# Turning keys and receptances as half-array blocks into one shared PSUM pair, in a fused linear-attention and token-mixing kernel

## The chip, the cores and the metric

The kernel runs on one core of a Trainium2 chip. The metric is the device time of one execution in microseconds (us), the median of the runs shown. Engines are named as in the profile: PE is TensorE (PEld its weight loads), DVE VectorE, ACT ScalarE, POOL GpSimd, SP the engine that issues most DMAs.

## The reference

The inputs are r, k, v and w of 4 batches, 8 heads, 768 steps and 48 channels, and a bonus u for each head and channel. A state of 48 by 48 is carried along the steps of each head:

```python
for t in range(S):
    cur = np.einsum('bhd,bhe->bhde', u[None] * kt, vt)
    y[:, :, t] = np.einsum('bhd,bhde->bhe', rt, state + cur)
    state = wt[:, :, :, None] * state + np.einsum('bhd,bhe->bhde', kt, vt)
```

The heads are then laid side by side to x (4 x 768 x 384), and a token mixer follows:

```python
wq = x @ w_q; wk = x @ w_k
W_tok = scale * np.einsum('bsd,btd->bst', wq, wk)
mixed = np.einsum('bst,btd->bsd', W_tok, x)
return (np.maximum(mixed, 0.0) @ w_out)
```

## The kernel before

Time is cut into chunks of C = 128 steps, and two chunks make a unit of 256 steps. Each of the 4 batches has three units, so there are twelve, numbered n = 0 to 11; n = 11 is the last ("end"). `unit(n, batch)` lists all steps of one. Even units use the first buffer of a ring of two, odd units the second, which is why names such as KT_107 and KT_108 alternate.

**Loads.** Four DMAs bring w, k, r and v (wg, kg, rg, vg, line 223), each into a ring of four buffers. ScalarE takes the logarithm of w (lw, 379); casts of k and r to bf16 (k16, r16, 389) and of v (VB, 493) run on GpSimd or ScalarE.

**Decays.** TensorE sums the logarithms with constant triangles (CM) into a wide buffer of two PSUM banks (cw); ScalarE makes ep (423) and en (428) of it, the exponentials of both signs.

**Turns.** `transposed` turns k16 and r16 with the identity: eight matmuls of 128 rows each, k into one bank (kt), r into another (rt), both 2 KB of bf16. VectorE or ScalarE copies k out (ks, 265 or 259); VectorE makes qT = r times ks (462), RT = r times ep (471), and KT = k times en (476), which may run on GpSimd from ks. The first and last unit make ep, en, RT and KT in halves, one for each chunk c.

**Within a chunk.** A = KT by RT is a wide buffer, masked by VectorE into AM (535). The matmuls "VB,AM" apply it to v; "SB,RT" add what the state gives. The state's update is kd (KT turned back, 261 or 267) by VB, and SB (602). The bonus goes by "UB,qT", dd, and Vd = dd times VB (515, GpSimd). X (670 on VectorE, 668 on ScalarE) is the sum in bf16; it is the mixer's x.

**Mixer.** X is turned to XT by TensorE and a copy, for units 9 and 10 by a DMA transpose from SP's queue (699). Then "wk,XT" and "XT,wq" with the copy QK, and after a batch's third unit T and TS, mx ("QK,TS"), the relu MX (271 or 273), the output matmuls "wo,MX", the copy os (259 or 265) and a store (803).

**What sets the order.** Each `add` records a step with the steps it needs. Nothing is scheduled at build time: `ORDER` is the list of all 642 steps in the order in which they are issued, and each engine gets its own steps in that order. `WAYS` holds one letter for each step that may run in more than one way: an engine (A, D, P), or for TensorE a form (E whole array, e or c in half-array pieces); a small d is VectorE reading PSUM directly. `BANKS` gives each PSUM buffer its first bank of eight; a wide one takes two. Waits between engines follow from the buffers. Every engine works strictly through its own list, so a waiting instruction holds all behind it; SP's queue of DMAs as well.

Of the kernel before, what the change touches and what calls it, by code (L numbers as in the profile page):

```python
# [10 lines left out]
F32 = mybir.dt.float32  # L11
# [21 lines left out]
class Plan:  # L33
# [86 lines left out]
]  # L120
WAYS = (
    "PPDDPDDDPDPDDPPPPPPDDPAPPEDddPPDAAcENDEDDAPEDdPAAEAEcEAEDAPPEDdAPAEDcNDEAAAAAAAADPPEAdPP"
    "AEAEEEAEDAPAcDPPADEAEcEAEAAPPcDdPPAEDcEAEADAAAAAAAPPcDdPPDEDccNDEAAPPcAdPPAeAEcNDEDAPPcD"
    "PPPDEDcEAEAAAADADAAPAcAdPPAEDEENDDPPcAdPPDeDccNDAPPcDPPPPDPPAcNDeAADNDEDDAADDDDDDAADAADN"
    "NNNNEEENNENNNENEEEENNEN"
)
BANKS = [
# [15 lines left out]
def kernel(  # L143
# [40 lines left out]
    def const(shape, dtype, name):  # L184
# [9 lines left out]
        wg=(4, HW, F32), rg=(4, HW, F32), kg=(4, HW, F32), vg=(4, HW, F32), os=(10, 2 * DM, F32),  # L194
# [51 lines left out]
    def bank():  # L246
        return Buf("s")
# [112 lines left out]

    def unit(n, batch):
# [57 lines left out]
        for cs in fine:  # L419
            w_ = 512 * len(cs)  # L420

            def f_ep(e, cs=cs):
                nc.scalar.activation(  # L423
                    view(ep.tile, cs[0] * EW + 1, [[2 * EW, NP], [EW, len(cs)], [1, C]]),
                    sums(cs), ACT.Exp, bias=kp, scale=1.0)

            def f_en(e, cs=cs):
                nc.scalar.activation(  # L428
                    view(en.tile, cs[0] * C, [[U, NP], [C, len(cs)], [1, C]]), sums(cs), ACT.Exp,
                    bias=km, scale=-1.0)  # L430
# [429 lines left out]
```

## Time and profile before

| | us |
|---|---|
| median of 3 runs (100.25 to 101.56) | 100.32 |
| the profiled execution | 99.53 |
| its span on the chip | 97.8 |
| of it 7.34 to 80.39: VectorE's first KT to the last unit's first X | 73.05 |
| of it 80.39 to 84.99: between the last unit's two halves of X | 4.60 |

The span begins with the first instruction that the profiler shows and ends with the last. TensorE's clock was granted in full throughout (1.00). In the profile's rows the engine stands first, then the operation with what it writes and reads; "128*128 128x48" on a matmul is the stationary tile (rows times columns) and what streams through it. A matmul's own length is its whole passage, and several overlap, so its price is read from start to start. In brackets stands the engine's idle time just before, and what ended it.

### The profile page before, as it was taken

Reading aid. Unit: us, or ns where it says so; the run is one execution under the profiler, and the core shown is the slowest. Engines: PE = TensorE matmul, PEld = TensorE weight load, DVE = VectorE, ACT = ScalarE, POOL = GpSimd, SP = SyncE. Lnnn points to the kernel's source line nnn. Section 1 sums busy time; section 2 is a strip of 40 time slices with the busy share of each in tenths; the row PEclk is TensorE's granted clock in tenths of the full one; section 3 lists DMA queues with packets and bytes.
Section 4 is the critical chain, followed back from the end, with each engine's and each line's share of the span. In section 5 each row is a group of like instructions: output and inputs, shape, how many; then the busy total and the mean of one; then the engine's idle time right before and its main releaser. Section 6 shows DMA issues by size and latency. Waiting matters only on the chain.

```text
span 97.8 us, 4074 instructions
## 1 busy us (share of the span) xinstructions
PE 87.7 (90%) x1710; PEld 67.6 (69%) x1713; DVE 81.7 (83%) x142; ACT 76.0 (78%) x112; POOL 68.1 (70%) x106
## 2 busy tenths in 40 slices
PE   4996888999889899999999999999999999998940
PEld 1354677878677798877788787897787776675410
DVE  5608989999999998999898999899998996384850
ACT  5237988889799799899999999869889856806610
POOL 6659758728799998767999998999968991000000
PEclk9999999999999999999999999999999999999999
DMA  1999999999999999999999999999913695928593
GB/s 29 304 323 325 325 325 299 222 292 315 287 306 247 227 287 215 304 270 245 303 301 308 277 300 294 311 323 248 289 57 132 195 153 150 397 83 322 215 319 112
DMA packets 54914, 25.03 MB, mean 256 GB/s; under 512 B 52592, under 2 KB 53744, under 8 KB 54896
## 3 DMA queue, kind: packets, MB, share of 16 engines
q1 hardware_dynamic: 54736, 24.58, 90.6%
q8 instruction: 13, 0.21, 0.8%
q10 hardware_dynamic: 160, 0.20, 0.6%
q14 instruction: 5, 0.04, 0.1%
HBM read 19.66 MB, written 4.72 MB: 249 GB/s over the span
## 4 chain that ended last, share of the span: by engine, by line
PE 42%; DMA 18%; POOL 18%; DVE 8%; issue 4%; ACT 3%; SPq 3%; POOLq 0%; DVEq 0%; ACTq 0%
PE PS L176 42%; DMA vg<-in_v_dram 12%; POOL VB L493 7%; POOL Vd L515 6%; DMA kg<-in_k_dram 6%; SPq L223 3%; DVE os L265 2%; POOL k L389 2%; POOL KT L476 2%; POOL r L389 2%; DVE RT L471 1%; ACT en L428 1%; DVE AM L535 1%; ACT ep L423 1%; DVE qT L462 1%
## 5 line engine op out<-in xcount | busy, mean ns | idle before, releaser
L535 DVE TENSOR_TENSOR AM<-PS,US 128x1024 bf16<-128x1024 f32 x24 | 28.8, 1218 | 1.0 <-PE PS L176 0.6
L493 POOL CAST VB<-vg 64x384 bf16<-64x384 f32 x42 | 21.1, 503 | 3.2 <-DMA vg<-in_v_dram 0.9
L515 POOL TENSOR_TENSOR Vd<-VB,dd 128x768 bf16<-128x768 bf16 (+1 forms) x14 | 18.0, 1292 | 1.6 <-DVE dd L265 1.1
L428 ACT ACTIVATE en<-PS,km 128x1024 bf16<-128x1024 f32 (+1 forms) x14 | 13.6, 989 | 2.4 <-PE PS L176 2.0
L423 ACT ACTIVATE ep<-PS,kp 128x1024 bf16<-128x1024 f32 (+1 forms) x14 | 13.8, 1003 | 1.4 <-PE PS L176 1.1
L176 PE MATMUL PS<-wo,MX 128*128 128x384 bf16 x72 | 13.5, 326 | 0.5 <-DVE MX L273 0.5
L176 PEld LDWEIGHTS <-KT 48*128 48x128 bf16 (+1 forms) x288 | 10.3, 95 | 3.9 <-issue 1.7
L389 POOL CAST k<-kg 128x768 bf16<-128x768 f32 x11 | 9.0, 824 | 4.5 <-DMA kg<-in_k_dram 4.3
L379 ACT ACTIVATE lw<-wg 128x768 bf16<-128x768 f32 x12 | 10.1, 844 | 2.2 <-DVE kd L230 2.1
L176 PE MATMUL PS<-RT,KT 48*128 48x128 bf16 x192 | 9.2, 217 | 1.2 <-DVE qT L462 0.5
L176 PE MATMUL PS<-CM,lw 64*128 64x128 bf16 (+1 forms) x160 | 9.4, 230 | 0.6 <-DVE ks L265 0.4
L176 PEld LDWEIGHTS <-MX 128*128 128x128 bf16 x72 | 6.2, 97 | 4.9 <-DVE MX L273 1.3
L476 DVE TENSOR_TENSOR KT<-PS,en 128x1024 bf16<-128x1024 bf16 (+1 forms) x10 | 6.3, 631 | 3.7 <-ACT en L428 3.6
L389 POOL CAST r<-rg 128x768 bf16<-128x768 f32 x10 | 8.2, 823 | 1.2 <-DMA rg<-in_r_dram 1.1
L271 ACT ACTIVATE MX<-PS 128x768 bf16<-128x768 f32 (+1 forms) x10 | 7.6, 780 | 1.5 <-PE PS L176 1.4
L471 DVE TENSOR_TENSOR RT<-PS,ep 128x1024 bf16<-128x1024 bf16 (+1 forms) x14 | 8.4, 610 | 0.5 <-PE PS L176 0.3
L462 DVE TENSOR_TENSOR qT<-PS,ks 128x1024 bf16<-128x1024 bf16 x12 | 8.2, 680 | 0.7 <-PE PS L176 0.7
L176 PEld LDWEIGHTS <-lw 64*128 64x128 bf16 (+1 forms) x160 | 6.8, 96 | 2.3 <-issue 0.9
L670 DVE TENSOR_TENSOR X<-PS,Vd 128x768 bf16<-128x768 f32 (+1 forms) x8 | 6.8, 850 | 1.6 <-PE PS L176 1.5
L176 PE MATMUL PS<-ID,r 128*128 128x128 bf16 x96 | 7.4, 220 | 0.8 <-POOL r L389 0.7
L176 PE MATMUL PS<-Z 128*128 128x512 bf16 x16 | 6.5, 523 | 1.2 <-DVE Z L826 1.2
L259 ACT COPY os<-PS 128x768 f32<-128x768 f32 (+1 forms) x9 | 6.2, 694 | 1.8 <-PE PS L176 1.8
(77 smaller groups left out, 189.7 us busy)
## 6 DMA issues: line engine op xcount, KB each, us to landing
wg<-in_w_dram SPq DMA_DIRECT2D x12, 384.0 KB, 5.3
kg<-in_k_dram SPq DMA_DIRECT2D x12, 384.0 KB, 6.0
rg<-in_r_dram SPq DMA_DIRECT2D x12, 384.0 KB, 5.1
vg<-in_v_dram SPq DMA_DIRECT2D x12, 384.0 KB, 5.9
out_dram<-os SPq DMA_DIRECT2D x9, 384.0 KB, 2.6
out_dram<-os SPq DMA_DIRECT2D x5, 192.0 KB, 2.6
wof<-in_moe_w_out_dram SPq DMA_DIRECT2D x1, 576.0 KB, 6.2
out_dram<-os ACTq DMA_DIRECT2D x1, 192.0 KB, 2.3
```

The lines of the kernel that those rows point to most:

```text
L176: return nc.tensor.matmul(o, l, rr, start=start, stop=stop, skip_group_check=True, is_transpose=trans)
L271: nc.scalar.activation(o, i, ACT.Relu)
L379: nc.scalar.activation(view(lw.tile, 0, [[64, H], [512, 2], [1, D]]), view(g["wg"].tile, 0, [[D2, H], [D, 2], [1, D]]), ACT.Ln, bias=0.0, ...
L389: op(view(o.tile, 0, [[64, H], [512, 2], [1, D]]), view(g[src].tile, 0, [[D2, H], [D, 2], [1, D]]))
L423: nc.scalar.activation(view(ep.tile, cs[0] * EW + 1, [[2 * EW, NP], [EW, len(cs)], [1, C]]), sums(cs), ACT.Exp, bias=kp, scale=1.0)
L428: nc.scalar.activation(view(en.tile, cs[0] * C, [[U, NP], [C, len(cs)], [1, C]]), sums(cs), ACT.Exp, bias=km, scale=-1.0)
L462: lambda e: nc.vector.tensor_tensor(qT.tile, at(rt, BF16), ks.tile, ALU.mult),
L471: nc.vector.tensor_tensor(slots(RT.tile, cs, C, 0, 64), slots(at(rt, BF16), cs, C, 0, 64), slots(ep.tile, cs, EW, 65, -65), ALU.mult)
L476: on("D" if e == "d" else e).tensor_tensor(plain(KT.tile, cs), plain(at(kt, BF16) if e == "d" else ks.tile, cs), plain(en.tile, cs), ALU.mult)
L493: op(view(VB.tile, c * DM, [[1, DM]], p0=half * 64, pn=64), view(g["vg"].tile, (1 - half) * D, [[D2, H], [1, D]], p0=c * 64, pn=64))
L515: (nc.vector if e == "D" else nc.gpsimd).tensor_tensor(Vd.tile[:, cols], VB.tile[:, cols], view(dd.tile, cs[0] * H, [[1, len(cs) * H], [0, ...
L535: AMs[c] = add(("AM", n, c), "D", lambda e, c=c, A=A: nc.vector.tensor_tensor(view(AM[c].tile, 0, [[C, 8], [1, C]]), view(at(A), 0, [[C, 8 ...
```

## The change

Four things are done, and the tables ORDER, WAYS and BANKS are replaced.

1. `transposed` writes k and r into one wide buffer `kr` of two banks. Each of the eight matmuls becomes two: rows 0 to 63 and rows 64 to 127 by turns, each with a 64 by 64 piece of the identity. Chunk 0 lies in the first bank, chunk 1 in the second; in each, a head pair's k stands beside its r. What reads them (ks, qT, RT, KT) steps over the other.
2. ep, en, ks, qT, RT and KT are laid out by chunk first and head pair second, where before it was the other way; the halves of the first and last unit become separate blocks.
3. The rings of wg, rg, kg and vg have five buffers for four.
4. The DMA transposes of X must be issued after the last unit's loads.

```diff
-        wg=(4, HW, F32), rg=(4, HW, F32), kg=(4, HW, F32), vg=(4, HW, F32), os=(10, 2 * DM, F32),
+        wg=(5, HW, F32), rg=(5, HW, F32), kg=(5, HW, F32), vg=(5, HW, F32), os=(10, 2 * DM, F32),
...
+        if end:
+            for x in turned_x:
+                x["after"] += [g[z + "L"] for z in ("wg", "kg", "rg", "vg")]
...
-                    view(ep.tile, cs[0] * EW + 1, [[2 * EW, NP], [EW, len(cs)], [1, C]]),
+                    view(ep.tile, cs[0] * NP * EW + 1, [[EW, NP], [NP * EW, len(cs)], [1, C]]),
...
-        kt, rt = bank(), bank()
-
-        def transposed(name, src, step, o):
+        kr = wide()
+
+        def transposed(name, src, step, z):
             def f(e):
-                x = at(o, BF16)
+                x = at(kr, BF16)
                 for hp in range(NP):
                     for j in range(2):
-                        mm(view(x, hp * U + (1 - j) * 64, [[C, 2], [1, 64]]),
-                           src.tile[:, ds(j * 512 + hp * 128, 128)], ID16, trans=True)
-            return add((name, n), "E", f, [step, su["ID"]] + new(name[0] + "16"), o, [src])
+                        for c in range(2):
+                            rows = ds(c * 64, 64)
+                            mm(x[:, ds((c * NP + hp) * U + z * C + (1 - j) * 64, 64)],
+                               src.tile[rows, ds(j * 512 + hp * 128, 128)], ID16[rows, rows],
+                               trans=True)
+            return add((name, n), "E", f, [step, su["ID"]] + new(name[0] + "16"), kr, [src], mode=1)
...
+        def turned(z, cs=(0, 1)):
+            return view(at(kr, BF16), cs[0] * NP * U + z * C, [[U, NP * len(cs)], [1, C]])
```

What the new table moves is shown at three places. First VectorE's list at the start, from the first KT to the second AM; KT, RT and the rest are the first unit's, AM the masked products. Before:

```order
L476 TENSOR_TENSOR KT_107<-PS,en_99 128x4x128 x2
L265 COPY ks_101<-PS 128x1024
L471 TENSOR_TENSOR RT_105<-PS,ep_97 128x4x128 x2
L462 TENSOR_TENSOR qT_103<-PS,ks_101 128x1024
L535 TENSOR_TENSOR AM_0_115<-PS,US 128x1024
L535 TENSOR_TENSOR AM_0_117<-PS,US 128x1024
```

And now:

```order
L488 TENSOR_TENSOR KT_111<-PS,en_103 128x512
L264 COPY ks_105<-PS 128x1024
L488 TENSOR_TENSOR KT_111<-PS,en_103 128x512
L483 TENSOR_TENSOR RT_109<-PS,ep_101 128x512
L473 TENSOR_TENSOR qT_107<-PS,ks_105 128x1024
L483 TENSOR_TENSOR RT_109<-PS,ep_101 128x512
L547 TENSOR_TENSOR AM_0_119<-PS,US 128x1024
```

The halves of KT and RT, which stood in pairs, are apart, with ks and qT between them.

Second, VectorE's list at the last unit, from the masked product of its second chunk over the two halves of X. Before:

```order
L535 TENSOR_TENSOR AM_1_118<-PS,US 128x1024
L670 TENSOR_TENSOR X_130<-PS,Vd_114 128x384
L265 COPY os_81<-PS 128x768
L602 TENSOR_TENSOR SB_122<-PS,ep_98 128x192
L265 CAST QK_132<-PS 128x256
L670 TENSOR_TENSOR X_130<-PS,Vd_114 128x384
```

And now:

```order
L547 TENSOR_TENSOR AM_1_122<-PS,US 128x1024
L682 TENSOR_TENSOR X_134<-PS,Vd_118 128x384
L264 CAST QK_136<-PS 128x256
L614 TENSOR_TENSOR SB_126<-PS,ep_102 128x192
L264 COPY XT_128<-PS 128x384
L682 TENSOR_TENSOR X_134<-PS,Vd_118 128x384
```

An output copy (os) is gone from between the halves, and the copy of the turned first half (XT) has come there. On TensorE the two groups of six "wo,MX" matmuls that stood between the last unit's two "VB,AM" groups now stand ahead of the first: 36 of the 72 come before it, where it was 24.

Third, SP's queue of DMAs behind the last load. Before:

```order
L223 DMA vg_78<-in_v_dram 128x8x96
L803 DMA out_dram<-os_80 128x768
L803 DMA out_dram<-os_82 128x768
L699 DMA_TRANSPOSE XT_124<-X_130 128x6x128
L803 DMA out_dram<-os_79 128x768
L699 DMA_TRANSPOSE XT_123<-X_130 128x6x128
L803 DMA out_dram<-os_81 128x768
```

And now:

```order
L222 DMA vg_79<-in_v_dram 128x8x96
L711 DMA_TRANSPOSE XT_127<-X_134 128x6x128
L711 DMA_TRANSPOSE XT_128<-X_134 128x6x128
L816 DMA out_dram<-os_83 128x768
L816 DMA out_dram<-os_88 128x768
L816 DMA out_dram<-os_85 128x768
```

Both transposes of X have moved ahead of all stores.

More of the change, by code (lines that the diff above doesn't have):

```diff
@@ L84 @@
 ORDER = [
[35 rows of a table removed]
[35 rows of a table added]
 ]
 WAYS = (
[L122 to L125, printed above, removed]
+    "PPDDDPPPPPPPDDPPDPAPPDAPPEDddPPDDAccNDEAAPAEAdPAAEDEENDEAAPPEDdPPDEAEEAEDAAAAAAAAAPEAPPP"
+    "DEDEEEAEDAAAEAdPPAEAEcEAEAAPAEDdPAAEDENDEADDAAAAAAPPcDdPPAEAEENDEDAPPcDdPADEDccEAEADPPEA"
+    "dPPDEDcNDEDAAAADAADPPcDPPPDEAEENDAPPcDdPAAEDccNDDPPcDdPPPDPPAcNDeDDANDEDADADAAADDDDDDAAE"
+    "NENNENNENEENEEENNNENEEN"
 )
 BANKS = [
[7 rows of a table removed]
[6 rows of a table added]
 ]
@@ L359, in bonus @@
                        reads=[z])
+    turned_x = []
     def unit(n, batch):
@@ L428, in f_en @@
                 nc.scalar.activation(
-                    view(en.tile, cs[0] * C, [[U, NP], [C, len(cs)], [1, C]]), sums(cs), ACT.Exp,
+                    view(en.tile, cs[0] * 512, [[C, NP], [512, len(cs)], [1, C]]), sums(cs), ACT.Exp,
                     bias=km, scale=-1.0)
@@ L436, in unit @@
                 eps[c], ens[c] = x, y
-        kt, rt = bank(), bank()
-        def transposed(name, src, step, o):
+        kr = wide()
+        def transposed(name, src, step, z):
             def f(e):
-                x = at(o, BF16)
+                x = at(kr, BF16)
                 for hp in range(NP):
                     for j in range(2):
-                        mm(view(x, hp * U + (1 - j) * 64, [[C, 2], [1, 64]]),
-                           src.tile[:, ds(j * 512 + hp * 128, 128)], ID16, trans=True)
-            return add((name, n), "E", f, [step, su["ID"]] + new(name[0] + "16"), o, [src])
+                        for c in range(2):
[4 more added lines that the diff above has]
+            return add((name, n), "E", f, [step, su["ID"]] + new(name[0] + "16"), kr, [src], mode=1)
         def plain(t, cs=(0, 1)):
-            return view(t, cs[0] * C, [[1, 1024]] if len(cs) > 1 else [[U, NP], [1, C]])
+            return view(t, cs[0] * 512, [[C, NP * len(cs)], [1, C]])
+        def turned(z, cs=(0, 1)):
+            return view(at(kr, BF16), cs[0] * NP * U + z * C, [[U, NP * len(cs)], [1, C]])
         def slots(t, cs, w_, x, step):
-            return view(t, cs[0] * w_ + x, [[(3 - len(cs)) * w_, NP * len(cs)], [step, 2], [1, 64]])
-        kTs = transposed("kT", k16, k16s, kt)
-        rTs = transposed("rT", r16, r16s, rt)
+            return view(t, cs[0] * NP * w_ + x, [[w_, NP * len(cs)], [step, 2], [1, 64]])
+        kTs = transposed("kT", k16, k16s, 0)
+        rTs = transposed("rT", r16, r16s, 1)
         ks = ring("ks")
-        kss = add(("ks", n), "AD", lambda e: copy(e, ks.tile, at(kt, BF16)), [kTs], ks, [kt],
+        kss = add(("ks", n), "AD", lambda e: copy(e, plain(ks.tile), turned(0)), [kTs], ks, [kr],
                   cols=1024)
@@ L461, in unit @@
         qTs = add(("qT", n), "D",
-                  lambda e: nc.vector.tensor_tensor(qT.tile, at(rt, BF16), ks.tile, ALU.mult),
-                  [rTs, kss], qT, [rt, ks])
+                  lambda e: nc.vector.tensor_tensor(plain(qT.tile), turned(1), plain(ks.tile),
+                                                    ALU.mult),
+                  [rTs, kss], qT, [kr, ks])
         RT, KT = ring("RT"), ring("KT")
@@ L476, in f_KT @@
                 on("D" if e == "d" else e).tensor_tensor(
-                    plain(KT.tile, cs), plain(at(kt, BF16) if e == "d" else ks.tile, cs),
+                    plain(KT.tile, cs), turned(0, cs) if e == "d" else plain(ks.tile, cs),
                     plain(en.tile, cs), ALU.mult)
-            x = add(("RT", n, cs[0]), "D", f_RT, [rTs] + [eps[c] for c in cs] + new("ep"), RT, [rt, ep],
+            x = add(("RT", n, cs[0]), "D", f_RT, [rTs] + [eps[c] for c in cs] + new("ep"), RT, [kr, ep],
                     cols=512 * len(cs), half=half)
@@ L482, in unit @@
                     cols=512 * len(cs), half=half,
-                    more=dict(P=([kss], [ks]), D=([kss], [ks]), d=([kTs], [kt])))
+                    more=dict(P=([kss], [ks]), D=([kss], [ks]), d=([kTs], [kr])))
             for c in cs:
@@ L531, in f_A @@
                         mm(x[:, ds(hh * 512 + hp * C, C)],
-                           KT.tile[ds(hh * 64, D), ds((2 * hp + c) * C, C)],
-                           RT.tile[ds(hh * 64, D), ds((2 * hp + c) * C, C)])
+                           KT.tile[ds(hh * 64, D), ds((c * NP + hp) * C, C)],
+                           RT.tile[ds(hh * 64, D), ds((c * NP + hp) * C, C)])
             As = add(("A", n, c), "E", f_A, [RTs[c], KTs[c]], A, [RT, KT], mode=1)
@@ L546, in f_kb @@
                         cp = c * NP + hp
-                        x = ds((2 * hp + c) * C, C)
+                        x = ds(cp * C, C)
                         if e == "E":
@@ L701, in unit @@
                     [xs], XT, [X])
+                turned_x.append(XTs)
             else:
```

8 lines of the change are left out of this document (4 added, 4 removed), and 83 rows, old and new, of tables (BANKS, ORDER).

## The prediction

> **What bounds the kernel now.** I read the page's busy shares first, then the windows, then VectorE's waits, then the timeline of the end. The page gives for each engine its busy time, share of the span and instructions.
>
> ```profile
> PE 87.7 (90%) x1710; PEld 67.6 (69%) x1713; DVE 81.7 (83%) x142; ACT 76.0 (78%) x112; POOL 68.1 (70%) x106
> ```
>
> No share decides alone, so I cut the span where VectorE's part of the work turns: at its first product of the first unit (KT, 7.34 us) and at the two halves of the last unit's X (80.39 and 84.99 us). The columns are length, then busy time and count of each engine, the granted clock, DMA share and GB/s.
>
> ```profile
> 7.34:80.39 73.05, 68.55 (x1526) 57.17 (x1529) 69.45 (x111) 65.56 (x95) 62.80 (x85) 1.00 1.00 265
> 80.39:84.99 4.60, 4.52 (x81) 3.09 (x80) 2.30 (x4) 3.32 (x6) 0.76 (x1) 1.00 0.77 272
> 84.99:97.80 12.81, 8.51 (x81) 4.70 (x78) 7.10 (x14) 4.27 (x10) 0.00 (x0) 1.00 0.59 219
> ```
>
> In the first 73.05 us VectorE (third figure) works 69.45 us: 95%, with 73.05 - 69.45 = 3.6 us idle. ScalarE has 7.5 us free there, GpSimd 10.3 us. TensorE's 68.55 us count each matmul's whole passage, and matmuls overlap, so it is not full. VectorE bounds this stage. In the second stretch TensorE is busy 4.52 of 4.60 us and VectorE half of it: TensorE's order bounds there. The rest is a chain of short steps through all engines. What VectorE waits for in the first stage (total, times, longest):
>
> ```profile
> DVE KT L476 <- ACT en L428: 3.6, 3, 3.1
> DVE dd L265 <- PE PS L176: 0.8, 2, 0.5
> DVE qT L462 <- PE PS L176: 0.7, 2, 0.5
> DVE AM L535 <- PE PS L176: 0.6, 3, 0.2
> DVE RT L471 <- PE PS L176: 0.3, 1, 0.3
> DVE RT L471 <- ACT ep L423: 0.2, 1, 0.2
> ```
>
> The 3.1 us of the first row lie ahead of 7.34. Of the rest 0.8 + 0.7 + 0.6 + 0.3 = 2.4 us are for TensorE. This is all that a quicker TensorE, earlier loads or a lighter GpSimd can give back in this stage, whatever they save themselves.
>
> **The turns of k and r.** Eight matmuls of 128 rows by 128 columns become sixteen of 64 rows by 64, on two halves of the array in turn, for 24 turns. From TensorE's timeline (start, length, form, count):
>
> ```profile
> 26.77 0.61 PE L176 MATMUL PS<-ID,k 128*128 128x128 bf16 x8
> 27.31 0.62 PE L176 MATMUL PS<-RT,KT 48*128 48x128 bf16 x16
> 40.31 0.61 PE L176 MATMUL PS<-CM,lw 64*128 64x128 bf16 x16
> 40.76 0.39 PE L176 MATMUL PS<-RT,KT 48*128 48x128 bf16 x8
> 49.22 0.62 PE L176 MATMUL PS<-ID,r 128*128 128x128 bf16 x8
> 49.68 0.77 PE L176 MATMUL PS<-VB,AM 128*128 128x48 bf16 x24
> 83.15 0.25 PE L176 MATMUL PS<-ID,X 64*128 64x64 bf16 x6
> L176 PE MATMUL PS<-ID,X 64*128 64x64 bf16 x6 | 0.2, 190 | 0.0
> ```
>
> A turn takes 49.68 - 49.22 = 0.46 us from start to start, 57 ns a matmul. The new form has a row, the last unit's X: six in 0.25 us, one of them 190 ns, so (0.25 - 0.19)/5 = 12 ns each. Sixteen take 0.20 us: 0.26 us less, times 24 is 6.2 us. The upper bound of the price is the half-row form with 128 columns (CM, lw): (40.76 - 40.31)/16 = 28 ns, 0.45 us a turn, which saves nothing. I take the row of the same shape.
>
> A change of array shape costs too: turn k to RT, KT (whole to half rows) takes 27.31 - 26.77 = 0.54 us where turn r to VB, AM (no change) took 0.46: 0.08 us. Counted through the order of instructions, between whole, half-row and half-column forms there are 102 changes before and 124 now: 22 x 0.08 = 1.8 us back. The Trainium skill, page TensorEngine Tiling (Array Packing), section Key Properties, says that changing the tiling mode drains the engine, a rule that speaks against this change; the trace agrees, with the 0.08 us just read.
>
> The table also chooses other forms. Three more units take the running sums (CM) on whole rows:
>
> ```profile
> 16.59 1.05 PE L176 MATMUL PS<-CM,lw 128*128 128x256 bf16 x8
> 17.47 0.34 PE L176 MATMUL PS<-UB,qT 128*128 128x2 bf16 x8
> ```
>
> That is 0.88 us against 0.45, so 3 x 0.43 = 1.3 us; sixteen more whole-row turns of KT at 57 ns, in place of 32 small ones at 12 ns, are another 0.5. TensorE's net is -6.2 + 1.8 + 1.8 = -2.6 us, with 0 to +3.6 if the halves gain nothing. It reaches the end only through the 2.4 us of waits above.
>
> **VectorE's own work.** By form (busy, mean ns), the rows whose counts change:
>
> ```profile
> L670 DVE TENSOR_TENSOR X<-PS,Vd 128x768 bf16<-128x768 f32 x6 | 5.7, 947 | 0.0
> L267 DVE TENSOR_SCALAR kd<-PS 128x768 bf16<-128x768 bf16 x3 | 1.6, 546 | 0.0
> L476 DVE TENSOR_TENSOR KT<-PS,en 128x512 bf16<-128x512 bf16 x2 | 0.8, 424 | 3.3 <-ACT en L428 3.3
> L265 DVE COPY dd<-PS 128x16 f32<-128x16 f32 x6 | 1.0, 168 | 0.8 <-PE PS L176 0.8
> L273 DVE TENSOR_SCALAR MX<-PS 128x384 bf16<-128x384 f32 x5 | 2.5, 548 | 1.0 <-PE PS L176 1.0
> L471 DVE TENSOR_TENSOR RT<-PS,ep 128x1024 bf16<-128x1024 bf16 x10 | 6.9, 687 | 0.3 <-PE PS L176 0.3
> L476 DVE TENSOR_TENSOR KT<-PS,en 128x1024 bf16<-128x1024 bf16 x8 | 5.5, 682 | 0.4 <-ACT en L428 0.3
> ```
>
> Ahead of the last unit's first X it gets one X (0.95), one kd (0.55), one half KT (0.42), one dd (0.17) and one TS, which has no row there; MX is a copy of the same 384 elements, 0.55. The sum is 2.64; neighbours overlap by some 0.07 each, so +2.3 us. The memsets of kd that leave VectorE lie ahead of 7.34, where it waits 3.1 us anyway, and count nothing. GpSimd has room for them: it waits 4.3 us for kg (quoted below), the first of it ahead of its first cast, so I take nothing. The new strided reads of the pair cost nothing: RT reads its bank in runs of 64 (687 ns) as fast as KT contiguous ones (682).
>
> **The start.** The first unit's halves of ep and en now lie in separate blocks.
>
> ```profile
> 9.14 0.76 DVE L471 TENSOR_TENSOR RT<-PS,ep 128x512 bf16<-128x512 bf16 x2 [0.20 <-ACT ep L423]
> 10.43 2.35 DVE L535 TENSOR_TENSOR AM<-PS,US 128x1024 bf16<-128x1024 f32 x2
> ```
>
> Both halves of RT waited for the second ep. In the new order the first is free of it: two KT, ks, RT, qT, RT are four of 0.42 and two of 0.68, 3.04 less overlaps, some 2.65 us, so AM can start at 10.0 in place of 10.43: -0.4 us (0 if TensorE is late with A).
>
> **The end.** Between the last unit's X halves VectorE waits 1.49 us for TensorE.
>
> ```profile
> 80.04 2.11 PE L176 MATMUL PS<-wo,MX 128*128 128x384 bf16 x12
> 82.08 0.27 PE L176 MATMUL PS<-SB,IDU 128*64 128x192 bf16 x2
> 80.39 0.56 DVE L670 TENSOR_TENSOR X<-PS,Vd 128x384 bf16<-128x384 f32 x1
> 81.28 0.96 DVE L265 COPY os<-PS 128x768 f32<-128x768 f32 x1 [0.33 <-PE PS L176]
> 84.99 0.56 DVE L670 TENSOR_TENSOR X<-PS,Vd 128x384 bf16<-128x384 f32 x1 [1.49 <-PE PS L176]
> ```
>
> TensorE does twelve output matmuls (wo, MX) in that gap, 82.08 - 80.04 = 2.04 us. In the new order these stand ahead of it, in the first stage, where TensorE's net relief of 2.6 covers them (without that cover they come back as waits of VectorE, 2.0). Two changes of shape go too. The gap shrinks by 2.1, from 4.60 to 2.5. VectorE's work in it, 2.30 of the second window, loses the os copy (0.96) and gains a copy of XT (some 0.4, as half a KT above): 1.7, the lower bound of the gap, 0.8 below what I take; the upper is 4.6. From the second X on, TensorE's list is the same, so I change nothing.
>
> **Loads and SP.** A fifth buffer lets a load start a unit sooner.
>
> ```profile
> POOL k L389 <- DMA kg<-in_k_dram: 4.3, 4, 1.8
> 72.31 4.05 SPq L803 DMA_DIRECT2D out_dram<-os  x2
> 76.46 1.37 SPq L699 DMA_TRANSPOSE XT<-X  x1
> 78.92 1.33 SPq L699 DMA_TRANSPOSE XT<-X  x1
> 82.26 12.72 SPq L803 DMA_DIRECT2D out_dram<-os  x11
> ```
>
> This frees GpSimd, which has 10.3 us of slack already; by itself it is worth nothing but its share of VectorE's waits. Both transposes of X now go ahead of all stores, so the three stores that left before 78.92 queue behind them. Eleven issues took 12.72 us with waits in them; the queue has room for three more before the last copy. Cost 0, at most the length of one such issue, 12.72/11 = 1.2.
>
> **Sum.** VectorE's work +2.3; its waits for TensorE halved, -1.2 (bounds 0 and -2.4, the middle because the relief of 2.6 is as large as the waits but most of it falls beside them); start -0.4; end -2.1. Together -1.4 us: 99.53 of the profiled execution (1.73 outside its span of 97.80) becomes 98.1, and the median of 100.32, which stands 0.79 above that execution, becomes 98.9. With waits and start at their bounds the sum is -2.6 to +0.2, and the case's own range 97.7 to 100.5.
>
> **Rivals.** *The waits vanish.* Loads, GpSimd and TensorE are all lighter, and VectorE's last 1.2 us of waits go as well: 97.7. For it: every wait has an upstream reason that the change touches. Against: with 2.3 us more work at 95% busy, small gaps of another cause arise. 0.24.
>
> *The waits stay.* They are lengths of single steps, not lack of TensorE: +2.3 - 0.4 - 2.1 = -0.2, 100.1. For it: 2.4 us in eight waits, none over 0.5. 0.20.
>
> *The halves don't overlap.* TensorE gets +3.6 us; if half of it shows on VectorE (+1.8), +1.6 in all, 101.9. Against it is the 12 ns of the row above. The Trainium skill, page TensorE: Matmul & The Clock Gate, section "Wait — 56ns, not 53.3ns?", has a floor of about 25 ns from start to start however small the matmul; by it a turn would take 0.40 us and this rival would hold, but the trace's 12 ns lies below it. 0.04.
>
> *The pair is held too long: slower.* Before, k's bank was free once ks (and KT) had read it, whatever became of r. Now k and r share two banks, and the next unit's turns wait for the last of ks, qT, RT and KT, with everything behind them in TensorE's queue, AM's and SB's matmuls among it. The nearest price is TensorE's wait for ks:
>
> ```profile
> PE PS L176 <- DVE ks L265: 0.8, 2, 0.5
> ```
>
> 0.4 us each; once a unit and seen in full by VectorE, 12 x 0.4 = 4.8: 98.9 + 4.8 = 103.7. It decides from 1.4 + 2.0 = 3.4 us, 0.28 a unit. Against: in the new order k's and r's turns of a unit stand close together and may use any of four pairs. 0.12.
>
> **How the numbers follow.** The forecast has 0.40. A measurement of this kernel can tell about 2%, 2.0 us, from no change: faster is below 98.3, slower above 102.3. Faster: 0.22 of the first rival and a quarter of the forecast's 0.40 (0.6 of its 2.8 us lie below 98.3), together 0.32. Slower: 0.09 of the last rival and 0.01 of the third, 0.10. Same: 0.58. The range goes from 0.8 below the first rival, the lower bound of the gap at the end, up to the third rival: 96.9 to 101.9; past it lie most of the last rival and little else.
>
> **What would show it.** Right: turns of k or r in about 0.2 us of TensorE's timeline; VectorE busy about 71.7 us from its first KT to the last unit's first X, with about 2 us idle; the X halves some 2.5 us apart; the first AM near 10.0. Wrong: VectorE's idle in that stage at 3.6 or more, TensorE waiting for ks, qT or RT ahead of turns, wk's matmuls in the gap waiting for the transposed XT, or a last store that waits in SP's queue.

## The result and the profile after

The changed kernel takes 105.43 us (median of four runs, 105.38 to 105.59) where the kernel before takes 100.28 on the same chip. The ratio of the runs is on record as 1.0545, 95% interval 1.0498 to 1.0593 (the two medians alone give 1.051). Some runs of a kernel are over 1.5% longer than its fastest; what is said below of times and medians leaves these out. The prediction was 98.9, with 96.9 to 101.9 as its range. The change is slower, and the sign of the forecast was wrong.

The head of the page after, and the windows cut at the same three points as before (first KT, the last unit's two halves of X; columns as in the prediction):

```profile
span 103.7 us, 4374 instructions
PE 88.2 (85%) x1857; PEld 66.0 (64%) x1861; DVE 81.1 (78%) x141; ACT 78.1 (75%) x114; POOL 66.5 (64%) x105
```

```profile
8.76:88.19 79.43, 70.77 (x1660) 56.32 (x1665) 71.55 (x116) 67.67 (x98) 58.97 (x79) 1.00 0.91 238
88.19:90.93 2.74, 2.66 (x74) 2.20 (x74) 1.50 (x6) 2.07 (x4) 0.00 (x0) 1.00 1.02 391
90.93:103.70 12.77, 8.57 (x78) 4.85 (x75) 6.60 (x13) 5.13 (x11) 0.00 (x0) 1.00 0.64 240
```

Set against the three rows of before, the 5.9 us of span divide without a remainder: the first KT comes 8.76 - 7.34 = 1.42 later; VectorE works 71.55 - 69.45 = 2.10 more in the first stage; it idles 79.43 - 71.55 = 7.88 there where it idled 3.60, so 4.28 more; the gap between the X halves is 1.86 shorter; the end is the same within 0.04. 1.42 + 2.10 + 4.28 - 1.86 - 0.04 = 5.90. This is bookkeeping along one engine, not yet a cause. What VectorE now waits for (total, times, longest):

```profile
DVE KT L488 <- PE PS L175: 4.8, 2, 2.6
DVE ks L264 <- PE PS L175: 2.6, 3, 1.0
DVE KT L488 <- ACT ep L428: 1.3, 1, 1.3
DVE AM L547 <- PE PS L175: 0.9, 3, 0.4
```

The waits of dd, qT, AM and RT that the prediction meant to halve did fall by nearly half, from 2.4 to 1.3 us (AM 0.9, dd and qT 0.2 each). But KT and ks, the two readers of k's half of the pair, had no wait for TensorE before, and now they have the longest. The place of the longest is unit 4, in the timeline (start, length, engine, operation):

```profile
29.94 0.83 ACT L394 CAST r<-rg 128x768 bf16<-128x768 f32 x1 [0.54 <-DMA rg<-in_r_dram]
29.96 0.41 PE L175 MATMUL PS<-ID,k 64*128 64x64 bf16 x16
30.19 0.28 PE L175 MATMUL PS<-SB,RT 48*128 48x48 bf16 x8
30.68 1.12 ACT L428 ACTIVATE ep<-PS,kp 128x1024 bf16<-128x1024 f32 x1
31.86 0.37 PE L175 MATMUL PS<-VB,kd 128*128 128x48 bf16 x8 [0.32 <-ACT ep L428]
32.16 0.41 PE L175 MATMUL PS<-ID,r 64*128 64x64 bf16 x16
32.68 0.69 DVE L488 TENSOR_TENSOR KT<-PS,en 128x1024 bf16<-128x1024 bf16 x1 [2.23 <-PE PS L175]
33.41 1.01 ACT L258 COPY ks<-PS 128x1024 bf16<-128x1024 bf16 x1 [1.60 <-DVE KT L488]
```

k's turn is over at 30.37 and en has been ready since 29.41, yet KT starts at 32.68, 0.11 us after the end of *r's* turn (32.16 + 0.41). r's turn is late because a product that waits for ep stands ahead of it on TensorE, and ep itself stands on ScalarE behind r's cast, which waited for r's load. The chain that ended last (start, length) shows the way from SP's queue of loads to KT:

```profile
22.54 1.46 SPq L222
...
24.04 5.83 DMA rg<-in_r_dram
...
30.68 1.13 ACT ep L428
...
31.86 0.73 PE PS L175 x24
...
32.68 0.69 DVE KT L488
```

Then ks, on ScalarE, waits until KT has read the same banks. So a reader of k waits for the last writer of the shared pair that is issued ahead of it, r's turn; and two readers on different engines take turns, which is not new with the pair, since ks and KT shared k's bank before too. The Trainium skill, page PSUM — Partial Sum Buffer, section "PSUM bank collisions raise a hardware error", has a rule that asks for such waits: two engines must not be on the same bank (and the same partitions) at once, reads against reads included, even at different addresses. The waits of the trace are as this rule asks; the prediction, which drew on two other pages, missed it.

The same lies behind the wait ahead of KT in unit 6 (1.25 us; the view names ep, r's turn ends at 47.55, KT starts at 47.66) and of most of that ahead of ks in unit 5 (1.02; k's turn ends at 38.65, r's at 39.43): 4.5 us with unit 4's. Two more waits ahead of ks look alike and are not. In unit 9 (0.74) k's own turn stood still for 0.79 us in the middle, from 65.83 on, which the profiles of e3 and e8 below don't show. In unit 11 (0.82) r's turn ends only 0.23 us behind k's, and with own banks the wait is still 0.79 (e1, below).

The start, from the same timeline:

```profile
4.45 1.17 POOL L229 MEMSET kd<- 128x1280 bf16 x1
5.68 0.29 POOL L284 TENSOR_SCALAR_AFFINE_SELECT CM<-CM 64x128 bf16<-64x128 bf16 x1
6.28 0.29 POOL L284 TENSOR_SCALAR_AFFINE_SELECT CM<-CM 64x128 bf16<-64x128 bf16 x1
6.62 0.92 PE L175 MATMUL PS<-CM,lw 128*128 128x256 bf16 x7 [1.04 <-POOL CM L284]
7.65 1.27 ACT L433 ACTIVATE en<-PS,km 128x512 bf16<-128x512 f32 x2 [2.48 <-PE PS L175]
8.24 0.41 PE L175 MATMUL PS<-ID,r 64*128 64x64 bf16 x16
8.76 0.42 DVE L488 TENSOR_TENSOR KT<-PS,en 128x512 bf16<-128x512 bf16 x1 [2.58 <-PE PS L175]
```

GpSimd writes the zeros of a kd buffer before it finishes the triangles CM; the running sums wait for CM, en for the sums, and KT, once en's first half is done at about 8.28, waits for r's turn again.

### The profile page after: what moved, and what is told of

Its sections match the earlier page's. It is cut to its first block, busy times and chain, and to the rows that moved or that the text cites. A ratio compares the mean times of both kernels' runs of the same rounds, so it can differ in the third digit from the quotient of the medians.

```text
span 103.7 us, 4374 instructions
## 1 busy us (share of the span) xinstructions
PE 88.2 (85%) x1857; PEld 66.0 (64%) x1861; DVE 81.1 (78%) x141; ACT 78.1 (75%) x114; POOL 66.5 (64%) x105
## 4 chain that ended last, share of the span: by engine, by line
PE 39%; SPq 22%; DVE 13%; issue 9%; DMA 6%; POOL 5%; ACT 3%; DVEq 0%; POOLq 0%; ACTq 0%
PE PS L175 39%; SPq L222 22%; DMA rg<-in_r_dram 6%; DVE AM L547 3%; POOL VB L505 3%; POOL k L394 2%; DVE KT L488 2%; DVE ks L264 1%; DVE RT L483 1%; DVE qT L473 1%; DVE SB L614 1%; ACT ep L428 1%; ACT VB L505 1%; DVE X L682 1%; ACT os L258 1%
## 5 line engine op out<-in xcount | busy, mean ns | idle before, releaser
L505 POOL CAST VB<-vg 64x384 bf16<-64x384 f32 x40 | 20.1, 503 | 3.5 <-DMA vg<-in_v_dram 2.1
L175 PE MATMUL PS<-CM,lw 64*128 64x128 bf16 (+1 forms) x136 | 10.5, 239 | 2.3 <-POOL CM L284 1.0
L258 ACT COPY os<-PS 128x768 f32<-128x768 f32 (+1 forms) x12 | 8.2, 692 | 4.2 <-PE PS L175 4.1
L175 PE MATMUL PS<-RT,KT 48*128 48x128 bf16 x192 | 9.7, 217 | 1.5 <-DVE RT L483 1.2
L175 PEld LDWEIGHTS <-lw 64*128 64x128 bf16 (+1 forms) x136 | 7.5, 95 | 4.5 <-issue 3.4
L394 POOL CAST r<-rg 128x768 bf16<-128x768 f32 x9 | 7.4, 824 | 2.4 <-DMA rg<-in_r_dram 2.1
L682 DVE TENSOR_TENSOR X<-PS,Vd 128x768 bf16<-128x768 f32 (+1 forms) x9 | 7.7, 862 | 1.2 <-PE PS L175 1.0
L394 POOL CAST k<-kg 128x768 bf16<-128x768 f32 x10 | 8.2, 824 | 0.7 <-DMA kg<-in_k_dram 0.6
L175 PE MATMUL PS<-VB,AM 128*128 128x48 bf16 x192 | 7.8, 183 | 0.6 <-DVE AM L547 0.5
L175 PE MATMUL PS<-ID,KT 128*128 128x128 bf16 x80 | 6.7, 220 | 1.3 <-DVE KT L488 0.9
```

What stands on the lines that cost most here:

```text
L175: return nc.tensor.matmul(o, l, rr, start=start, stop=stop, skip_group_check=True, is_transpose=trans)
L258: nc.scalar.copy(o, i)
L394: op(view(o.tile, 0, [[64, H], [512, 2], [1, D]]), view(g[src].tile, 0, [[D2, H], [D, 2], [1, D]]))
L505: op(view(VB.tile, c * DM, [[1, DM]], p0=half * 64, pn=64), view(g["vg"].tile, (1 - half) * D, [[D2, H], [1, D]], p0=c * 64, pn=64))
```

## The experiments

**Theory 1**: sharing one pair makes k's readers wait for r's turn. **Theory 2**: the kd zeros on GpSimd delay the start. **Theory 3**: VectorE's longer list costs its 2.1 us. The rival to all is the new order as such. Each run stood beside runs of the kernel before on its chip; the ratio is to these, with its 95% interval. The kernel before varied between 99.5 and 101.9 there, so ratios and trace intervals are read rather than medians where less than 1 us matters.

| run | median us | ratio | interval |
|---|---|---|---|
| changed kernel | 105.43 | 1.0545 | 1.0498 to 1.0593 |
| e1 own banks | 102.31 | 1.0211 | 1.0112 to 1.0311 |
| e2 own banks, zeros on VectorE | 102.64 | 1.0232 | 1.0146 to 1.0317 |
| e3 zeros on VectorE | 104.49 | 1.0425 | 1.0346 to 1.0504 |
| e4 r's turn later, units 4 and 6 | 103.76 | 1.0372 | 1.0268 to 1.0476 |
| e5 own banks in six units | 102.87 | 1.0247 | 1.0129 to 1.0365 |
| e6 order of before, halves in 3 units | 117.03 | 1.1653 | 1.1553 to 1.1753 |
| e7 before, end in another order | 105.04 | 1.0446 | 1.0313 to 1.0578 |
| e8 four load buffers | 105.42 | 1.0467 | 1.0330 to 1.0605 |
| e9 before, new layouts, five buffers | 101.26 | 1.0103 | 0.9995 to 1.0210 |
| e10 e1, work back on ScalarE | 106.34 | 1.0743 | 1.0606 to 1.0881 |
| e11 e3 and e4 together | 102.32 | 1.0237 | 1.0132 to 1.0343 |
| e12 e2, v loaded once | 101.53 | 1.0138 | 1.0075 to 1.0200 |
| e13 all cures of order | 101.53 | 1.0073 | 1.0033 to 1.0114 |
| e14 e1 without four kd | 102.17 | 1.0148 | 1.0068 to 1.0228 |
| e15 changed, without four kd | 105.14 | 1.0387 | 1.0312 to 1.0461 |
| e16 e13, v loaded once | 100.78 | 1.0069 | 1.0027 to 1.0110 |
| e17 before, v loaded once | 99.39 | 0.9824 | 0.9712 to 0.9936 |
| e18 e14 without four turns of KT | 102.17 | 1.0193 | 1.0129 to 1.0258 |

### Sharing: e1, e4, e5

e1 undoes the sharing, and with it the half turns; the order stays, and what reads the banks follows (the edit in short):

```diff
-        kr = wide()
+        kr = [bank(), bank()]
...
-                        for c in range(2):
-                            rows = ds(c * 64, 64)
-                            mm(x[:, ds((c * NP + hp) * U + z * C + (1 - j) * 64, 64)],
-                               src.tile[rows, ds(j * 512 + hp * 128, 128)], ID16[rows, rows],
+                        mm(view(x, hp * C + (1 - j) * 64, [[NP * C, 2], [1, 64]]),
+                           src.tile[:, ds(j * 512 + hp * 128, 128)], ID16,
```

> The changed kernel's order of steps, engines, five load buffers and chunk-first layouts, but k's and r's turns go into a bank of their own each (the two banks of the pair), with whole 128-row turns as before. Theory 1 (k's readers wait for r's turn because both lie in one pair of banks; the waits in the changed trace are 2.2 us in unit 4, 1.25 in unit 6, 1.0, 0.7 and 0.8 before the ks copies of units 5, 9 and 11, sum 6.0): about 100.3 us (99.3 to 101.5), and those five waits for TensorE gone, though each turn is 0.26 us longer again. Rival (the new order itself, or the loads, cost the time): 104.5 to 106.

102.3: 3.1 us of the 5.1 expected. Its window of the first stage, and its two rows of waits (line numbers moved):

```profile
8.28:85.71 77.43, 74.20 (x1494) 59.27 (x1493) 72.29 (x117) 68.17 (x98) 59.32 (x79) 1.00 0.92 248
```

```profile
DVE ks L266 <- PE PS L177: 1.1, 2, 0.8
...
DVE KT L497 <- PE PS L177: 0.8, 3, 0.4
```

Behind the first KT, the waits of KT and ks fall from 2.2 + 2.6 + 1.3 = 6.1 us to 1.9; ahead of it VectorE still idles 2.23 us for 2.58, now for en. Unit 4's wait falls from 2.23 to 0.22, unit 6's from 1.25 to 0.38, unit 5's from 1.02 to 0.33: 3.6 us in all, close to the 3.1 us of time. Unit 11's stays at 0.79, which the expectation had counted as gone. The order alone is not to blame: the same order is 3 us faster with own banks, although every turn is longer again. VectorE's idle falls by less, 7.88 to 77.43 - 72.29 = 5.14: other waits appear.

e4 keeps pair and half turns and moves two steps in ORDER:

```diff
-    ... 156, 207, 231, 235, 245, 204, 232, 319, ...
+    ... 156, 207, 235, 245, 204, 232, 231, 319, ...
...
-    ... 257, 292, 328, 291, 293, 326, 325, 162, 332, 329, ...
+    ... 257, 292, 291, 293, 326, 325, 162, 332, 329, 328, ...
```

(231 and 328 are r's turns of units 4 and 6, 232 and 329 the ks behind which they now stand.)

> The changed kernel, shared pair and half turns kept, with r's turn of units 4 and 6 put behind the copy ks of the same unit, so that KT and ks read k's half of the pair before r's turn writes the other. Theory 1: the KT waits of 2.2 and 1.25 us go, RT behind it pays up to 0.8 us each for the later turn: about 103.5 us (102.6 to 104.5). Rival (KT waits for something else that r's turn only happens to end with): 105.0 to 106.

103.8, 1.7 less. The KT of units 4 and 6 in its timeline, which started at 32.68 and 47.66:

```profile
30.33 0.69 DVE L488 TENSOR_TENSOR KT<-PS,en 128x1024 bf16<-128x1024 bf16 x1
...
44.59 0.69 DVE L488 TENSOR_TENSOR KT<-PS,en 128x1024 bf16<-128x1024 bf16 x1 [0.22 <-ACT en L433]
```

2.35 and 3.07 us earlier, and in unit 6 what KT now waits for is en. In unit 4 r's turn itself starts at 32.12, where it started at 32.16; only KT no longer waits for it. Moving r's turn of two units and nothing else removes both waits, so it was r's turn that held KT: theory 1 holds in its mechanism, and in size for these two units.

e5 gives own banks only to units 0, 4, 5, 6, 9 and 11 (`own = n in (0, 4, 5, 6, 9, 11)`):

> The changed kernel with own banks and whole turns only in the six units where the trace shows k's readers waiting for r's turn (0, 4, 5, 6, 9, 11); the shared pair and the half turns stay in the other six (1, 2, 3, 7, 8, 10). Theory 1, in place (only where r's turn stands between k's turn and k's readers does the sharing cost): the same as with own banks everywhere, 102.3 us, or up to 0.6 less (101.5 to 102.7). Rival (sharing costs everywhere a little, by banks held longer): 103.5 to 104.5.

102.9 lies just above the expected range and below the rival's; its ratio of 1.025 is e1's 1.021 within the intervals, and below the changed kernel's. The six units hold most of the loss, though units 9 and 11 were chosen on waits that were hardly for r's turn. "Up to 0.6 less" for the shorter turns in the other six was not seen.

### The start: e3, e2, e12

```diff
-    ... 14, 21, 32, 12, 1, ...
+    ... 14, 21, 31, 32, 12, 1, ...
```

(31 and 32 are the kd zeros, their letters in WAYS changed from P to D.)

> The changed kernel with one thing of the start undone: the zeros of the two kd buffers are written by VectorE in its idle stretch from 2.1 to 5.9 us, not by GpSimd ahead of the last two masks. Theory 2 (GpSimd's list holds the masks, these the cumulative sums, these the first KT): the first KT starts 1.3 us earlier, near 7.4 us, and the time is about 104.2 us (103.9 to 104.6). Rival (the lead is lost again in a later wait for a load or for TensorE): first KT earlier, time 105.2 to 105.5.

104.5, 0.9 less. Its start:

```profile
6.68 1.27 ACT L433 ACTIVATE en<-PS,km 128x512 bf16<-128x512 f32 x2 [1.53 <-PE PS L175]
6.82 0.82 POOL L394 CAST r<-rg 128x768 bf16<-128x768 f32 x1 [0.35 <-DMA rg<-in_r_dram]
7.70 0.41 PE L175 MATMUL PS<-ID,r 64*128 64x64 bf16 x16 [0.46 <-POOL r L394]
8.21 0.42 DVE L488 TENSOR_TENSOR KT<-PS,en 128x512 bf16<-128x512 bf16 x1 [1.66 <-PE PS L175]
```

en comes 0.97 us earlier, as theory 2 says, but KT only 0.55: it now waits for r's turn, that for r's cast, that for r's load. The sharing carries the load of r into KT.

> Both in one: own banks with whole turns, and the kd zeros on VectorE, in the changed kernel's order. Theories 1 and 2 together, added: about 99.0 us (98.0 to 100.3). If only theory 1 holds: 100.3. If only theory 2: 104.2. If neither: 105.4.

102.6: with own banks the zeros bring nothing. The first KT is at 7.82 for 8.28, but unit 1's KT at 15.06 for 14.69. Between them two waits for loads have grown:

```profile
11.54 0.84 ACT L386 ACTIVATE lw<-wg 128x768 bf16<-128x768 f32 x1 [1.20 <-DMA wg<-in_w_dram]
...
12.78 2.15 POOL L514 CAST VB<-vg 64x384 bf16<-64x384 f32 x4 [2.98 <-DMA vg<-in_v_dram]
```

e12 takes eleven loads away:

```diff
+            if name == "vg" and n:
+                g[name] = vg0[0]
+                g[name + "L"] = add((name, n), "S", None)
+                continue
```

> The changed order with own banks and the kd zeros on VectorE (102.6 us), with v loaded for unit 0 alone: the other eleven units use unit 0's v, so eleven of the 48 loads (4.3 of 18.9 MB) are left out and the output is that of repeated values. Theory (the early start is lost because the first units' loads queue behind each other): the first KT stays near 7.8 us, the waits for wg and vg between 10 and 16 us go, and the time is 101.4 us (100.6 to 102.0). Rival (loads are never on the path): 102.3 to 103.0.

The time is 101.5, as expected, but not all on the way there: the first KT is at 7.13, not near 7.8, and the cast of v (VB) shown above still waits 2.02 us, for unit 0's v. From unit 5's KT to the last X, e12 and e1 in one row each:

```profile
38.03:87.04 49.01, 48.34 (x1027) 38.70 (x1027) 44.79 (x74) 42.18 (x63) 33.17 (x43) 1.00 0.49 143
```

```profile
39.45:88.48 49.03, 48.37 (x1027) 38.72 (x1027) 44.79 (x74) 42.19 (x63) 33.30 (x43) 1.00 0.82 229
```

At a DMA share of 0.49 for 0.82 this stretch is no shorter; e2's is as long (39.87 to 88.89). Unit 2's KT starts at 19.29 in e12, 20.71 in e1 and 21.12 in e2, so the lead of 1.42 us over e1 is there by then. In these kernels the loads count only ahead of that point, and a lead won there is kept in full.

### Order alone: e11, e13, and e16, e17

> The changed kernel, shared pair and half turns kept, with both cures of order: the kd zeros on VectorE and r's turn of units 4 and 6 behind ks. If the two add (each alone gave 0.9 and 1.7): 102.8 us (102.4 to 103.2). Theory (the earlier start is used up in the first units, which wait for their loads): 103.5 us (103.2 to 104.2).

102.3, below both ranges: the two cures add up, and a little more. The start was not used up here.

e13 adds four moves: r's turn of unit 0 (49) behind its second KT (55), that of unit 5 (272) ahead of a turn of X (159), unit 4's SB (248) ahead of unit 5's ks (273), unit 11's turns (545, 546) ahead of T (437).

```diff
-    ... 271, 159, 272, 273, 248, 275, ...
+    ... 271, 272, 159, 248, 273, 275, ...
...
-    ... 527, 529, 437, 522, 545, 546, 177, ...
+    ... 527, 529, 545, 546, 437, 522, 177, ...
```

> The changed kernel with shared pair and half turns, cured by order alone: kd zeros on VectorE and r's turn of units 4 and 6 behind ks (together 102.3 us measured), and besides r's turn of unit 0 behind unit 0's KT, r's turn of unit 5 ahead of the turn of X that stood between, the SB of unit 4 ahead of unit 5's ks, and unit 11's two turns ahead of the sum T over X. Theory 1 for what is left (the waits of 1.6, 1.1 and 0.8 us before KT of unit 0 and ks of units 5 and 11 are still r's turn): they fall by 0.3, 0.5 to 1.0 and 0.7, the time to 100.8 us (100.0 to 101.7). Rival (what is left over the kernel before is not sharing): 101.9 to 102.8.

101.5, and 1.007 times the kernel before: inside what was expected, and 0.047 of the 0.0545 is gone with the pair and the half turns still there. The profiled execution took 103.05, above the others, so only its start is read:

```profile
7.13 0.42 DVE L488 TENSOR_TENSOR KT<-PS,en 128x512 bf16<-128x512 bf16 x1 [0.62 <-ACT en L433]
...
8.21 0.72 PE L175 MATMUL PS<-ID,r 64*128 64x64 bf16 x16 [0.45 <-DVE ks L264]
```

The first KT is at 7.13, ahead of the kernel before (7.34). This was the best version with the pair; no version with all its work in it beat the kernel before.

> The changed kernel cured by order alone (101.4 us, and its casts and copies now wait 18 us in all for loads, on several engines side by side, where the kernel before waits 7), with v loaded for unit 0 alone; the other units use unit 0's v, eleven of 48 loads are left out. Theory (with the waits for r's turn gone, the loads set what is left): 99.8 us (99.2 to 100.6). Rival (loads are waited for only where there is time): 101.0 to 101.8.

> The kernel before with the same eleven loads of v left out (the other units use unit 0's v). Theory (its order waits for loads 7 us in all, 1.3 of it for v, beside other work): 100.2 us (99.4 to 100.7), so the loads are not what sets its time. Rival (both kernels are paced by the loads): 98.0 to 99.2.

e16 has e13's ratio (1.0069 and 1.0073): by it no gain, though its median lies between the two ranges. So in the cured kernel the loads don't set what is left. e17 lies at the border of its two. Its ratio is 0.982, but against the four shortest runs of the kernel before beside it (99.78 to 100.45, median 100.19) e17 gains only 0.8 us. So what the kernel before gains from lighter loads is open between under 1% and 2%, and neither range is confirmed.

### VectorE's list: e10, e14, e15, e18

> The changed order with own banks and whole turns (102.3 us), and three pieces of VectorE's added work back on ScalarE (the copy TS of unit 5, kd of units 1 and 3: 0.56 + 0.55 + 0.55 = 1.65 us of VectorE, 2.1 us of ScalarE), the cast of wo back on GpSimd (1.14 us of ScalarE). Theory 3 (what is left over the kernel before is VectorE's longer list, which has few gaps): 100.9 us (100.4 to 101.6). Rival (the list is paced by TensorE or the loads, the pieces only turn into waits): 102.0 to 103.

Three letters D in WAYS became A, and the cast of wo P. 106.3, far on the other side; in part this is a fault of the experiment, the cast of wo came late.

```profile
70.77 1.14 POOL L266 CAST wo<-wof 128x1152 bf16<-128x1152 f32 x1
...
71.97 1.14 PE L177 MATMUL PS<-wo,MX 128*128 128x384 bf16 x6 [2.14 <-POOL wo L266]
```

TensorE, and all behind it, stood 2.1 us; what else this run lost is open. But ahead of that it says something: unit 8's KT starts at 59.20, in e1 at 59.16, with two of the three pieces (the copies kd of units 1 and 3) already gone from VectorE. To take work away without giving it to another engine, e14 and e15 leave out four copies:

```diff
             def f_kd(e, cs=cs):
+                if n in (3, 5, 7, 8):
+                    return
```

> The changed order with own banks and whole turns (102.3 us), with the copies kd of units 3, 5, 7 and 8 left out of VectorE (4 x 0.55 = 2.2 us) and given to no other engine; the state of those units is then built from an older kd. Theory 3 (VectorE's list is what the stage waits for, each us of it counts): 100.2 us (99.6 to 100.9). Rival (the engines wait for one another, work taken from one alone turns into waits): 101.6 to 102.6.

> The changed kernel itself, with the same four copies kd left out of VectorE (2.2 us), the state of those units built from an older kd. If VectorE's work counts one for one also beside the waits for r's turn: 103.2 us (102.8 to 103.8). Rival (the stage is set by the chain of casts, turns and KT, VectorE's list has the room): 104.6 to 105.6.

From unit 2's KT to the last X, e14 and then e1:

```profile
19.86:87.61 67.75, 66.11 (x1394) 53.69 (x1394) 61.25 (x97) 59.45 (x85) 50.64 (x65) 1.00 0.90 246
```

```profile
20.71:88.48 67.77, 66.12 (x1394) 53.70 (x1394) 62.64 (x101) 59.15 (x85) 49.95 (x65) 1.00 0.89 244
```

Four copies of 0.55 us fewer (VectorE is busy 61.25 us for 62.64), 0.02 us gained: theory 3 falls for own banks. For the changed kernel the times alone are less sharp: e15 is 0.3 us shorter by the median, 1.6% by the ratios (1.0387 for 1.0545, the kernel before being slower in that round). The traces settle it from unit 4's KT to the last X, where three of the four copies lie. First e15, then e8, which is the changed kernel with four load buffers:

```profile
32.04:89.69 57.65, 53.28 (x1282) 42.58 (x1283) 51.32 (x83) 48.58 (x72) 39.96 (x53) 1.00 0.85 223
33.22:90.90 57.68, 53.29 (x1282) 42.65 (x1283) 52.10 (x86) 48.60 (x72) 39.90 (x53) 1.00 0.87 226
```

Three copies fewer, 0.03 us gained: theory 3 falls here too. (e3 takes 57.68 us for this stretch as well; the profiled execution of the changed kernel takes 58.25, with the stop of 0.79 us in unit 9.) In e14's stretch TensorE is busy 66.1 of 67.8 us, so the last run also left out the turns of KT that fed those copies:

> As the run before it with own banks, whole turns and without the copies kd of units 3, 5, 7 and 8, and now without the turns of KT (kb) that fed them: 32 matmuls, 4 x 0.46 = 1.8 us of TensorE, are left out too; the state of those units is built from an older kd. From unit 2's KT to the last X TensorE is busy 66.1 of 67.8 us in that version. Theory (with own banks TensorE's list sets the pace): 100.3 us, 1.8 less (99.8 to 100.8), and that stretch 66.0 us. Rival (TensorE's busy time counts passages that overlap, another chain sets it): 101.7 to 102.4, the stretch 67.3 to 67.8.

```profile
21.13:88.49 67.36, 64.83 (x1370) 52.62 (x1370) 61.26 (x97) 59.06 (x85) 49.14 (x64) 1.00 0.87 238
```

67.36 for 67.75 us: 0.4 of the 1.8 (TensorE's busy time falls by 1.3). The rival holds: TensorE's list by itself doesn't set the pace either.

### What was kept or not: e8, e9, e6, e7

> The changed kernel with four load buffers of each kind again. Theory (the loads follow the TensorE and VectorE work, five buffers bring nothing): 105.4 us (105.0 to 105.9). Rival (the new order of loads needs the fifth buffer, SyncE's queue stands behind a load that waits for its buffer): 106.3 to 108.

105.42, the changed kernel's own time: the fifth buffer does nothing in it.

> The order, engines and banks of the kernel before, whole turns into own banks, with what is left of the change: five load buffers of each kind and the chunk-first layouts of KT, RT, ks, qT, ep and en. Theory (these two are worth nothing, the whole difference is sharing, order and engines): the time of the kernel before, 100.5 us (99.9 to 101.3). Rival (the layouts or the buffers cost or save): more than 1.0 away from it.

101.3, a ratio of 1.010 that reaches from 1.00 to 1.02: layouts and buffers gain nothing; whether they cost up to 2% this run can't tell.

> The order and engines of the kernel before, with all else of the change: five load buffers, chunk-first layouts, and k and r turned as halves into a shared pair in units 0, 3 and 6, where that order has r's turn behind k's readers and the banks have room for it; own banks and whole turns elsewhere (the banks are dealt out anew). Theory (halves, layouts and buffers are worth nothing by themselves; order and coupling made the difference): 100.3 us (99.7 to 101.0). Rival (half turns free TensorE where something waits for it, six turns of 0.26 us): 98.7 to 99.3. Rival (the layouts or the pair cost time of their own): 101.5 and more.

117.0, a miss that tells nothing of half turns. The pairs had no room among the banks as dealt, so all were dealt out anew, and TensorE then waited for VectorE where it had waited little before (for AM none is listed):

```profile
PE PS L177 <- DVE AM L556: 7.0, 6, 2.0
PE PS L177 <- DVE qT L482: 2.0, 2, 1.3
```

That the new dealing is behind these waits is argued, not shown: half turns in three units, layouts and buffers changed with it.

> The kernel before with nothing changed but the order from the last unit's first X on: the two products of MX with wo (2.1 us of TensorE) that stand between the last unit's two X move behind the second, one behind each wait of TensorE there, and two later ones move behind the next. The prediction's term for the end (X to X 4.6 to 2.5 us, not given back behind it): 98.5 us (97.8 to 99.3). Rival (TensorE is the bound behind the second X too, so 2.3 us of products come back there): 100.0 to 100.8, with X to X at 2.5 to 3.0 all the same.

105.0. In this kernel unit 2's MX is overwritten by unit 6's before its product reads it, so part of the output is not the reference's. Its two windows at the end:

```profile
81.98:85.54 3.56, 2.83 (x64) 2.05 (x63) 1.33 (x3) 2.47 (x5) 0.61 (x1) 1.00 0.61 183
85.54:103.30 17.76, 11.18 (x99) 6.07 (x96) 8.02 (x15) 5.14 (x10) 0.00 (x0) 0.99 0.53 201
```

The gap shrinks by 1.04, and what follows the second X grows from 12.81 to 17.76, by 4.95 us where the products that moved take 2.1. That is neither range: the places chosen for them cost more than the products, so the run can't tell whether they would be free behind the second X elsewhere.

## Why the prediction was wrong, point by point

**VectorE's waits: the step that failed.** "Its waits for TensorE halved, -1.2", within 0 and -2.4. In all they grew: idle 3.60 to 7.88 us, which the prediction had named as a sign of being wrong. The rows that it added up did fall as forecast, by 1.1 of 2.4 us; what the sum had at nothing were new waits. The bound was drawn from waits that the trace of before shows, and a new dependence, k's readers on r's turn, can't be among them. It cost 4.5 us of waits in units 4, 5 and 6. e4 shows the cause for units 4 and 6, e1 and e13 that it and its like account for most of the loss.

**The rival on the pair** had the place (the shared pair) and came nearest to the time (103.7), with a chance of 0.12, but another mechanism: the next unit's turns held by the last reader. It was the same unit's k that waited, for a writer that it does not need. "k's and r's turns of a unit stand close together", which I gave against it, is not so in unit 4: 29.96 and 32.16.

**The start.** "GpSimd has room for them ... so I take nothing" failed: the first KT came 1.42 us later, and the first AM at 11.29 in place of the 10.0 forecast. The room lies behind the masks, not ahead of them. The split RT itself did what was said: first KT to first AM is 2.53 us (8.76 to 11.29) for 3.09.

**VectorE's work.** +2.3 forecast, +2.10 measured: right as a sum of durations, wrong as a term of the time: e14 takes four copies off and gains 0.02 us, e15 three in the stretch read and gains 0.03. "VectorE bounds this stage", read from 95% busy, was not shown by it. That the term stood beside waits of opposite sign hid this.

**The turns.** Right: k's turn of unit 4 takes 30.19 - 29.96 = 0.23 us from start to start (0.20 forecast, 0.46 before). The halves overlap, and that rival is out. TensorE's net of -2.6 can't be read from the windows, since the output matmuls of the gap moved into the first stage with it; its busy time there rose by 2.2. By rows, busy time of the 24 turns is 10.0 us, with whole turns in the same order (e1) 14.7:

```profile
L175 PE MATMUL PS<-ID,k 64*128 64x64 bf16 x192 | 5.1, 191 | 0.9 <-issue 0.8
L175 PE MATMUL PS<-ID,r 64*128 64x64 bf16 x192 | 4.9, 191 | 0.0
```

**The end, SP, loads, layouts.** Right: the gap shrank by 1.86 (2.1 forecast), the end stayed at 12.77, five buffers are worth nothing (e8). That the layouts cost nothing is open within 2% (e9). What the output matmuls moved out of the gap cost in the first stage no run separates.

**Open.** What sets the pace of the own-bank version and the last 0.7% of e13: neither VectorE's list (e14), TensorE's (e18) nor the loads (e12, e16) alone. The page of e1 puts 63% of the chain that ended last on TensorE and 13% on VectorE, so the chain passes from one list to another. That several tight lists hold each other is argued from this, not shown. Half turns with a pair of banks each for k and r were not tried.

## What to carry to other kernels

When two buffers are put into one bank, list for each reader the last write into that bank issued ahead of it, and the loads and casts behind that write: these are the reader's new waits, and the profile of before can't show them. Here most of the cure was order, the second write behind the readers of the first, not giving up the shared bank. And a busy share of 95% is no price: leave a piece of work out and see whether the time follows before counting it in a sum.

## What was not expected of the hardware

Two engines that only read one bank also took turns here: in unit 4 ks on ScalarE, idle for 1.60 us, started 0.04 us after KT on VectorE had ended. The profile reads such waits from the program's semaphores; what the chip would do without them was not tried. The same zeros of a kd buffer took 1.17 us on GpSimd and 0.59 on VectorE, which wrote them as half as many 4-byte words. How the eight banks are dealt out may be worth more than any change of the work: e6, with its banks dealt anew, was 16.5% slower than the kernel before with the same sums to compute; the half turns, layouts and buffers in it were not separated from the dealing.
